# A four-layer attention and gated-MLP kernel: 17 query blocks over one unpadded token axis, and the bulk weights moved to another DMA queue and a later time

## Chip, cores, metric

One NeuronCore of a Trainium2 chip. The metric is device time in microseconds (us), median of several executions without the profiler. Profiles are of one separate execution each; their span is close to the timed figure, except where said. "Landing" is the moment when the last byte of a transfer has arrived; the "granted clock" is the share of its full rate at which PE was allowed to run.

KB is 1024 bytes, as the profile counts. Engine names in the profile: PE is the matrix engine, PEld its weight loads, DVE the vector engine, ACT the scalar engine, POOL and SP the others. Loads are issued by SP or ACT into that engine's own DMA queue.

## The reference

Four layers on 2048 tokens of width 448, in bf16: attention (A), gated MLP (B), A, B, each with a layernorm before it and a residual after it. The code is shortened here.

```python
def _A_ref(x, wqkv, wo):            # 16 heads of 28; each token sees itself and 7 others, 2 apart
    ...
    off = jnp.arange(8) * 2
    idx = pos[:, None] - off[None, :]          # keys pos, pos-2, ..., pos-14
    ...                                        # gather, scale, mask idx < 0, softmax, weighted sum
    return o @ wo

def _B_ref(x, w_gate, w_up, w_down):           # 448 -> 1792 -> 448
    return ((x @ w_gate) * (x @ w_up)) @ w_down

x = x + _A_ref(_layernorm(x), A_wqkv, A_wo)
x = x + _B_ref(_layernorm(x), B_w_gate, B_w_up, B_w_down)
x = x + _A_ref(_layernorm(x), A_wqkv, A_wo)
x = x + _B_ref(_layernorm(x), B_w_gate, B_w_up, B_w_down)
```

## The kernel before

Tokens are reordered (even ones, then odd ones), so that "2 apart" becomes "next to each other" inside each half of 1024. The work is cut into 16 blocks of 128 tokens and 4 chunks of 512. A static scheduler inside the kernel program takes all operations with their dependencies, priorities and estimated durations, and fixes one order for each engine. Each engine gets its operations in that order, and one that waits holds up those behind it (SP's 25.2 us below are a case).

The attention of a half runs in query blocks of at most 120, each with 8 keys in front, over an axis with 16 columns of padding before each half (cuts marked by dots, comments added, the settings of the last line gathered from several):

```python
QB, NQP, NQB, PAD = 120, 9, 18, 16
...
def qb_info(qb):
    r, k = divmod(qb, NQP)
    t0 = QB * k
    nq = min(QB, HALF - t0)                    # the ninth block of a half has 64 queries
    return r, k, t0, nq, nq + 8, HALF * r + t0
...
PE_T = ("00", "01")                            # layer 0, chunks 0 and 1: transposed by PE; the rest by DMA
HEAD_P = (-30.0, -29.5, -29.0, -28.5)          # priorities of the four chunks' layernorms of layer 0
HOLD_BA, LN1, ATT_P, A_CAP = 3000.0, (4,), 1.1, 6
```

The three MLP weights (1568 KB each) are loaded once, from SP, right after the small weights:

```python
for nm, lo, src in (("wg", 0, B_w_gate), ("wu", 64, B_w_up)):
    plain_dma("sp", WGU[lo:lo + 64, :, :], src.rearrange("(k p) f -> p k f", p=64), nm, f"d_{nm}", lat=26000.0, prio=-44)
plain_dma("sp", WD[:], B_w_down.rearrange("(c p) e -> p c e", p=128), "wd", "d_wd", lat=30000.0, prio=-43)
```

Chunks 2 and 3 of layer 0 are transposed by DMA, also from SP. In layer 0 these transposes wait until the last weight (`wd`) has landed:

```python
# xn_sb: the normalised block (a ring of 6 slots);  X: its transpose, xnTa
sc.add("sp", one(lambda E, ...: E.dma_start_transpose(X[:, :, c0:c0 + 128], xn_sb[:, slot, 0:128 * nt]), ("T", li, B)),
       1300.0, deps=[("xn", li, B)] + war + ([f"c_p0", "c_p1"] if par == 0 else []) + (["wd"] if li == 0 else []), ...)
```

From xnTa come Q and K (weights WQK) and V (weights WV); then scores, exponential (ACT, into E_sb), mask (DVE), weighted sum, normalisation, output projection. MLP matmuls read xnTb and WGU, then hT and WD. Most matmuls run as pairs, each on half of PE's rows.

The softmax here doesn't subtract the row's maximum and nothing guards it: scores larger than these inputs give would overflow.

## Time and profile before

| | before |
|---|---|
| time | 411.28 us (410.95 to 411.81, 4 runs beside those of the changed kernel) |
| span of the first profile | 814.9 us: PE at half rate in that execution |
| span of a second profile, taken with the experiments | 410.0 us: PE at full rate |
| PE busy in the second profile | 397.1 us (97%) |

The page, first two lines (span, then busy time of each engine, share of the span, and instructions):

```profile
span 814.9 us, 10679 instructions
...
PE 805.7 (99%) x4682; PEld 280.6 (34%) x4682; DVE 283.2 (35%) x561; ACT 213.6 (26%) x338; POOL 5.4 (1%) x21
```

The span is twice the timed figure, and PE is busy for 99% of it, longer than a timed execution takes in all. So the PE durations of this profile are useless for the timed run. SP's waits (what it waited for: us in all, times, longest) and then the page's DMA issues (queue, KB each, median us from issue to landing) of the same profile:

```profile
SPq L345 <- DMA WD<-in_B_w_down_dram: 25.2, 1, 25.2
```

```profile
WGU<-in_B_w_gate_dram SPq DMA_DIRECT2D x1, 1568.0 KB, 14.2
WGU<-in_B_w_up_dram SPq DMA_DIRECT2D x1, 1568.0 KB, 22.3
WD<-in_B_w_down_dram SPq DMA_DIRECT2D x1, 1568.0 KB, 26.0
...
xnTa<-xn_sb SPq DMA_TRANSPOSE x24, 2.5
```

SP stands still for 25.2 us on WD, and then transposes that land in 2.5 us each. It looks like 25 us to be gained. But it is SP that waits, and the question is whether PE needs those transposes earlier. The half-rate profile can't tell, as its PE is late for everything. The second profile of the same kernel answers: first its busy line, then PE's timeline around the spot (start, us, instructions; in brackets the idle time before, if any, and what ended it), then the transposes in a window around the head (shortest/median/longest issue in ns, first and last start):

```profile
PE 397.1 (97%) x4682; PEld 194.2 (47%) x4682; DVE 277.3 (68%) x561; ACT 209.9 (51%) x338; POOL 5.4 (1%) x21
```

```profile
49.00 0.33 PE L700 MATMUL ps<-qk 28*72 28x64 bf16 x16 [0.60 <-ACT E_sb L707]
49.27 6.36 PE L580 MATMUL ps<-xnTa,WQK 64*128 64x512 bf16 x56
...
64.35 1.69 PE L795 MATMUL ps<-xnTb,WGU 64*128 64x512 bf16 x14
```

### The profile page before, as it was taken

The page shows a single profiled execution, that of the slowest core. Times are in us where ns is not written, and L with a number is a line of the kernel's source. Part 1 is how long each engine was busy: PE and PEld are TensorE (multiplying, and loading weights), DVE is VectorE, ACT ScalarE, POOL GpSimd, SP SyncE. Part 2 cuts the span into 40 slices and gives each one's busy share as a digit, 9 for nine tenths or more (in the row PEclk, how much of TensorE's full clock was granted, in tenths as well). Part 3 has the DMA queues.
Part 4 walks back from the last instruction along what each step waited for, and adds up shares of the span by engine and source line. Part 5 has one row for each costly group of instructions (what it writes and reads, how often), then busy time and mean ns, then how long its engine had stood idle before and what let it go on. Part 6 is the DMA issues. An engine that isn't in the chain of part 4 may idle for free.

```text
span 814.9 us, 10679 instructions
## 1 busy us (share of the span) xinstructions
PE 805.7 (99%) x4682; PEld 280.6 (34%) x4682; DVE 283.2 (35%) x561; ACT 213.6 (26%) x338; POOL 5.4 (1%) x21
## 2 busy tenths in 40 slices
PE   9999999999999999999999999999999999999998
PEld 5323333333233333333333333333333333333333
DVE  5346335335522334333442343423234332211211
ACT  2465334421221213322142321323114101100110
POOL 2000000000000000000000000000000000000000
DMA  9811103000300201000310002100030020000000
GB/s 253 176 27 23 37 0 46 2 1 8 64 0 1 46 1 27 1 1 1 46 27 1 1 1 46 27 1 0 7 63 2 1 57 12 0 1 23 1 0 23
DMA packets 51750, 21.44 MB, mean 26 GB/s; under 512 B 43576, under 2 KB 50808, under 8 KB 51704
## 3 DMA queue, kind: packets, MB, share of 16 engines
q1 hardware_dynamic: 50984, 19.78, 12.1%
q8 instruction: 37, 0.61, 0.3%
q10 hardware_dynamic: 720, 0.98, 0.3%
q14 instruction: 9, 0.07, 0.0%
HBM read 8.43 MB, written 1.84 MB: 13 GB/s over the span
## 4 chain that ended last, share of the span: by engine, by line
PE 99%; DVE 1%; ACT 0%; issue 0%
PE ps L795 45%; PE ps L596 27%; PE ps L580 19%; PE ps L731 2%; PE ps L700 2%; PE ps L816 1%; PE ps L466 1%; PE ps L543 0%; DVE E_sb L713 0%; PE ps L727 0%; DVE x_sb L768 0%; DVE v_sb L680 0%; DVE st L513 0%; ACT E_sb L707 0%; DVE oT L751 0%
## 5 line engine op out<-in xcount | busy, mean ns | idle before, releaser
L795 PE MATMUL ps<-xnTb,WGU 64*128 64x512 bf16 x1568 | 373.9, 671 | 1.3 <-ACT E_sb L707 1.1
L795 PEld LDWEIGHTS ps<-xnTb,WGU 64*128 64x128 bf16 x1568 | 115.8, 142 | 230.8 <-issue 225.8
L596 PE MATMUL ps<-WD,hT 64*128 64x448 bf16 x840 | 177.4, 617 | 0.1
L801 ACT ACTIVATE g_sb<-ps 128x512 bf16<-128x512 f32 x112 | 66.8, 597 | 355.0 <-PE ps L795 354.9
L804 DVE TENSOR_TENSOR hT<-g_sb,ps 128x512 bf16<-128x512 bf16 x112 | 76.7, 685 | 219.5 <-ACT g_sb L801 219.4
L580 PE MATMUL ps<-xnTa,WQK 64*128 64x512 bf16 x448 | 108.8, 672 | 0.1
L596 PEld LDWEIGHTS ps<-WD,hT 64*128 64x128 bf16 x840 | 63.6, 147 | 102.1 <-issue 100.0
L768 DVE TENSOR_TENSOR x_sb<-x_sb,ps 128x448 bf16<-128x448 bf16 x62 | 36.2, 615 | 138.0 <-PE ps L596 138.0
L707 ACT ACTIVATE E_sb<-ps 128x960 bf16<-128x960 f32 (+1 forms) x72 | 64.4, 926 | 29.3 <-PE ps L700 29.1
L596 PE MATMUL ps<-wo_g,oT 64*128 64x448 bf16 x256 | 58.5, 603 | 0.9 <-DVE oT L751 0.8
L580 PE MATMUL ps<-WV,xnTa 64*128 64x448 bf16 (+1 forms) x280 | 56.4, 550 | 0.5
L580 PEld LDWEIGHTS ps<-xnTa,WQK 64*128 64x128 bf16 x448 | 32.4, 142 | 64.0 <-issue 59.6
L713 DVE TENSOR_TENSOR E_sb<-E_sb,MK 128x960 bf16<-128x960 bf16 (+1 forms) x72 | 44.3, 628 | 22.2 <-ACT E_sb L707 22.1
L631 ACT ACTIVATE qk<-ps 128x1024 bf16<-128x1024 f32 x24 | 24.5, 1023 | 77.6 <-PE ps L580 77.6
L513 DVE BATCH_NORM_STATS2 st<-x_sb 128x6 f32<-128x448 bf16 x64 | 37.1, 612 | 3.3 <-DMA x_sb<-in_A_x_dram 3.3
L534 DVE TENSOR_SCALAR xn_sb<-x_sb,mv,rstd 128x512 bf16<-128x512 bf16 (+1 forms) x64 | 32.9, 572 | 6.4 <-ACT rstd L518 6.4
L596 PEld LDWEIGHTS ps<-wo_g,oT 64*128 64x128 bf16 x256 | 17.3, 129 | 36.2 <-issue 33.3
L580 PEld LDWEIGHTS ps<-WV,xnTa 64*128 64x128 bf16 (+1 forms) x280 | 17.5, 127 | 34.3 <-issue 26.6
L742 ACT ACTIVATE R_sb<-R_sb 128x480 f32<-128x480 f32 (+1 forms) x32 | 18.4, 574 | 37.8 <-DVE R_sb L740 37.8
L680 ACT ACTIVATE v_sb<-ps 128x896 bf16<-128x896 f32 (+1 forms) x16 | 13.2, 822 | 48.0 <-PE ps L580 48.0
L751 DVE TENSOR_TENSOR oT<-ps,R_sb 128x480 bf16<-128x480 f32 (+1 forms) x36 | 22.3, 622 | 5.5 <-ACT R_sb L744 5.4
L740 DVE LOAD_MASK_SELECT R_sb<-ps x32 | 0.4, 14 | 64.5 <-PE ps L731 64.5
(45 smaller groups left out, 191.9 us busy)
## 6 DMA issues: line engine op xcount, KB each, us to landing
x_sb<-in_A_x_dram SPq DMA_DIRECT2D x4, 448.0 KB, 6.8
out_dram<-x_sb SPq DMA_DIRECT2D x15, 112.0 KB, 1.7
WGU<-in_B_w_gate_dram SPq DMA_DIRECT2D x1, 1568.0 KB, 14.2
WGU<-in_B_w_up_dram SPq DMA_DIRECT2D x1, 1568.0 KB, 22.3
WD<-in_B_w_down_dram SPq DMA_DIRECT2D x1, 1568.0 KB, 26.0
hT<-in_A_wqkv_dram ACTq DMA_DIRECT2D x4, 224.0 KB, 5.3
xnTb<-xn_sb SPq DMA_TRANSPOSE x32, 3.0
WV<-in_A_wqkv_dram SPq DMA_DIRECT2D x4, 112.0 KB, 5.4
```

The costliest lines, as they stand in the source:

```text
L513: sc.add("dve", one(lambda E, B=B: E.bn_stats(st6[:, B, :], x_sb[:, B, :]), ("bn", li, B)), 525.0, deps=[("x", li - 1, B)] + ([("xn", li - ...
L534: sc.add("dve", one(lambda E, B=B, dst=dst, src=src: E.tensor_scalar(dst, src, mv[:, B, 0:1], rstd[:, B:B + 1], ALU.subtract, ALU.mult), ( ...
L580: parts[0 if s < 3 else 1][1].append((lambda E, w=w, c=c, lo=lo, st=st, sp_=sp_: E.matmul(u["out"](w), u["lhs"](w, c, lo, lo + 64), u["rhs ...
L596: ins.append((lambda E, w=w, c=c, lo=lo, st=st, sp_=sp_: E.matmul(outs(w), lhs(w, c, lo), rhs(w, c, lo), start=st, stop=sp_), keys[w] if s ...
L631: return E.activation(dst, src, ACT.Copy) if hasattr(E, "activation") else E.tensor_copy(dst, src)
L707: return E.activation(E_sb[0:nk, slot, 2 * hp:2 * hp + 2, 0:4 * nq], ps[0:nk, b0:b0 + 2, 0:4 * nq], ACT.Exp, scale=SCALE)
L713: return E.tensor_tensor(e, e, m, ALU.mult)
L751: return E.tensor_tensor(oT[:, :, t0:t0 + nq], ps[:, bk[0], 0:4 * nq].rearrange("p (h n) -> p h n", h=4), R_sb[:, rs, 0:4 * nq].rearrange( ...
L768: sc.add("dve", one(lambda E: E.tensor_tensor(x_sb[:, B, :], x_sb[:, B, :], ps[:, bk[w], 0:D], ALU.add), ("x", li, B)), dve_est(D), deps=[ ...
L795: ins.append((lambda E, u=u, k=k, w=w: E.matmul(u["out"](w), WGU[64 * w:64 * w + 64, k, 128 * u["fc"]:128 * u["fc"] + 128], X[64 * w:64 * ...
L801: sc.add("act", one(lambda E, gs=gs, bk=bk: E.activation(g_sb[:, gs, :], ps[:, bk[0], :], ACT.Copy), ("G", li, j, fc)), act_est(512), deps ...
L804: sc.add("dve", one(lambda E, gs=gs, bk=bk, fc=fc: E.tensor_tensor(hT[:, fc, hs, :], g_sb[:, gs, :], ps[:, bk[1], :], ALU.mult), ("H", li, ...
```

## The change

Three things at once:

1. **17 query blocks** per attention layer over one axis of 2048 tokens without padding: the first of 128 queries, then 16 of 120, one of which straddles the middle and gets a mask of its own (and its last multiply cut in two). 28 V matmuls fewer, pads and their memsets gone.
2. **Bulk weights on ACT's queue, later.** They are gated on the normalisation of block 11, the last of chunk 2, so that chunk 2's transposes may go first. The transposes don't wait for `wd` any more. The intent is to bring chunk 2's transposes forward by a dozen us.
3. **Settings** of the scheduler: layernorms of chunks 2 and 3 at later priorities (the lowest number goes first), finer layernorm groups, a smaller lead for attention in the order (`ATT_P`), and two limits of the scheduler.

```diff
-HEAD_P = (-30.0, -29.5, -29.0, -28.5)
+HEAD_P = (-30.0,-29.5,-19.3,-18.8)
-HOLD_BA = 3000.0
+HOLD_BA = 2000.0
-LN1 = (4,)
+LN1 = (1,1,2)
-ATT_P = 1.1
-A_CAP = 6
+ATT_P = 0.6
+A_CAP = 5
 ...
 def qb_info(qb):
-    r, k = divmod(qb, NQP)
-    t0 = QB * k
-    nq = min(QB, HALF - t0)
-    return r, k, t0, nq, nq + 8, HALF * r + t0
+    if qb == 0:
+        return 0, 128, 0, 128
+    tok = 128 + QB * (qb - 1)
+    return tok - 8, 128, tok, QB
 ... (masks, buffers without pads, the straddling block: cut)
+    GATE = [("x", -1, 15)] if "02" in PE_T else [("xn", 0, 11)]
     for nm, lo, src in (("wg", 0, B_w_gate), ("wu", 64, B_w_up)):
-        plain_dma("sp", WGU[...], ..., nm, f"d_{nm}", lat=26000.0, prio=-44)
-    plain_dma("sp", WD[:], ..., "wd", "d_wd", lat=30000.0, prio=-43)
+        plain_dma("act", WGU[...], ..., nm, f"d_{nm}", deps=GATE, lat=12000.0 if lo == 0 else 20000.0, prio=-44)
+    plain_dma("act", WD[:], ..., "wd", "d_wd", deps=GATE, lat=26000.0, prio=-43)
 ...
-        1300.0, deps=[("xn", li, B)] + war + ([f"c_p0", "c_p1"] if par == 0 else []) + (["wd"] if li == 0 else []), ...
+        1300.0, deps=[("xn", li, B)] + war, ...
```

More of the change, by code (lines that the diff above doesn't have):

```diff
@@ L19 @@
 QB = 120
-NQP = 9
-NQB = 2 * NQP
-PAD = 16
-SEG = PAD + HALF
-CP = 2 * SEG
+NQB = 17
+EW = 4 * 128
 SCALE = DH ** -0.5
@@ L30 @@
 MAIN = "R64"
-PE_T = ("00", "01")
+PE_T = ("00","01")
 HEAD_LN = 4
-HEAD_P = (-30.0, -29.5, -29.0, -28.5)
+HEAD_P = (-30.0,-29.5,-19.3,-18.8)
 HOLD_A = 500.0
-HOLD_BA = 3000.0
+HOLD_BA = 2000.0
 HOLD_BB = 0.0
@@ L42 @@
 POOL_WQK = True
-LN0 = (2, 2)
-LN1 = (4,)
+LN0 = (2,2)
+LN1 = (1,1,2)
 VFIRST = False
@@ L49 @@
 JITTER = 0.0
-ATT_P = 1.1
-A_CAP = 6
+ATT_P = 0.6
+A_CAP = 5
 B_CAP = 8
 SEQ = "A00 A01 B10 A02 B11 A03 B12 A20 B13 A21 B30 A22 B31 A23 B32 B33".split()
-def col(tok):
-    return PAD + tok + (PAD if tok >= HALF else 0)
 def qb_info(qb):
-    r, k = divmod(qb, NQP)
-    t0 = QB * k
-    nq = min(QB, HALF - t0)
-    return r, k, t0, nq, nq + 8, HALF * r + t0
+    if qb == 0:
+        return 0, 128, 0, 128
+    tok = 128 + QB * (qb - 1)
+    return tok - 8, 128, tok, QB
+STRADDLE = next(q for q in range(NQB) if qb_info(q)[2] < HALF < qb_info(q)[2] + qb_info(q)[3])
 class Op:
@@ L391, in build @@
     eps_sb = sb([128, 1], dt.float32, "eps_sb")
-    xnT = {0: sb([128, 4, CP], bf, "xnTa"), 1: sb([128, 7, 1024], bf, "xnTb")}
-    qk = sb([128, 2, 4, CP], bf, "qk")
+    xnT = {0: sb([128, 4, S], bf, "xnTa"), 1: sb([128, 7, 1024], bf, "xnTb")}
+    qk = sb([128, 2, 4, S], bf, "qk")
     WQK = sb([128, 4, 2, 512], bf, "WQK")
@@ L399, in build @@
     v_sb = sb([128, NV, 512], bf, "v_sb")
-    E_sb = sb([128, NE, 4, 480], bf, "E_sb")
-    R_sb = sb([128, NR, 480], dt.float32, "R_sb")
+    E_sb = sb([128, NE, 4, EW], bf, "E_sb")
+    R_sb = sb([128, NR, EW], dt.float32, "R_sb")
     g_sb = sb([128, NG, 512], bf, "g_sb")
@@ L405, in build @@
     ones32 = sb([128, 32], bf, "ones32")
-    MK = sb([128, 2, QB], bf, "MK")
+    MK = sb([128, 3, 128], bf, "MK")
     ident = sb([128, 128], bf, "ident")
@@ L452, in build @@
     sc.add("pool", one(lambda E: E.memset(WQK[:].rearrange("p c w (h e) -> p (c w h) e", e=32)[:, :, DH:32], 0.0), "c_wqk0"), 700, prio=-45)
-    memset("pool", xnT[0][:, :, 0:PAD], 0.0, "c_p0", 150)
-    memset("pool", xnT[0][:, :, SEG:SEG + PAD], 0.0, "c_p1", 150)
     sc.add("pool", one(lambda E: E.memset(v_sb[:].rearrange("p s (h e) -> p (s h) e", e=32)[:, :, DH:32], 1.0), "c_v"), 400, prio=-40)
-    memset("pool", qk[:, :, :, 0:PAD], 0.0, "c_p2", 200)
-    memset("pool", qk[:, :, :, SEG:SEG + PAD], 0.0, "c_p3", 200)
     memset("pool", MK[:], 1.0, "i_mk0", 300)
-    sc.add("pool", one(lambda E: E.affine_select(MK[:, 0, :], MK[:, 0, :], [[-1, QB]], ALU.is_ge, 0.0, base=-1, channel_multiplier=1), "i_mk1"), 300, deps=["i_mk0"], prio=-40)
-    sc.add("pool", one(lambda E: E.affine_select(MK[:, 0, :], MK[:, 0, :], [[1, QB]], ALU.is_ge, 0.0, base=W, channel_multiplier=-1), "i_mk2"), 300, deps=["i_mk1"], prio=-40)
-    sc.add("pool", one(lambda E: E.affine_select(MK[:, 1, :], MK[:, 0, :], [[0, QB]], ALU.is_ge, 0.0, base=-8, channel_multiplier=1), "c_mk"), 300, deps=["i_mk2"], prio=-40)
+    sc.add("pool", one(lambda E: E.affine_select(MK[:, 0, :], MK[:, 0, :], [[-1, 128]], ALU.is_ge, 0.0, base=7, channel_multiplier=1), "i_mk1"), 300, deps=["i_mk0"], prio=-40)
+    sc.add("pool", one(lambda E: E.affine_select(MK[:, 0, :], MK[:, 0, :], [[1, 128]], ALU.is_ge, 0.0, base=0, channel_multiplier=-1), "c_mk0"), 300, deps=["i_mk1"], prio=-40)
+    sc.add("pool", one(lambda E: E.affine_select(MK[:, 1, :], MK[:, 1, :], [[-1, 128]], ALU.is_ge, 0.0, base=-1, channel_multiplier=1), "i_mk2"), 300, deps=["i_mk0"], prio=-39)
+    sc.add("pool", one(lambda E: E.affine_select(MK[:, 1, :], MK[:, 1, :], [[1, 128]], ALU.is_ge, 0.0, base=W, channel_multiplier=-1), "c_mk1"), 300, deps=["i_mk2"], prio=-39)
+    qx, kx = HALF - qb_info(STRADDLE)[2], HALF - qb_info(STRADDLE)[0]
+    sc.add("pool", one(lambda E: E.tensor_copy(MK[:, 2, :], MK[:, 1, :]), "i_mk3"), 300, deps=["c_mk1"], prio=-38)
+    sc.add("pool", one(lambda E: E.affine_select(MK[:, 2, qx:], MK[:, 2, qx:], [[0, 128 - qx]], ALU.is_ge, 0.0, base=-kx, channel_multiplier=1), "c_mk2"), 300, deps=["i_mk3"], prio=-38)
     memset("pool", ones32[:], 1.0, "c_ones", 100)
@@ L481, in build @@
         plain_dma("sp", dst, src, ("wo", j), "d_wo", deps=["c_wo"], lat=12000.0, prio=-45)
+    GATE = [("x", -1, 15)] if "02" in PE_T else [("xn", 0, 11)]
     for nm, lo, src in (("wg", 0, B_w_gate), ("wu", 64, B_w_up)):
-        plain_dma("sp", WGU[lo:lo + 64, :, :], src.rearrange("(k p) f -> p k f", p=64), nm, f"d_{nm}", lat=26000.0, prio=-44)
-    plain_dma("sp", WD[:], B_w_down.rearrange("(c p) e -> p c e", p=128), "wd", "d_wd", lat=30000.0, prio=-43)
+        plain_dma("act", WGU[lo:lo + 64, :, :], src.rearrange("(k p) f -> p k f", p=64), nm, f"d_{nm}", deps=GATE, lat=12000.0 if lo == 0 else 20000.0, prio=-44)
+    plain_dma("act", WD[:], B_w_down.rearrange("(c p) e -> p c e", p=128), "wd", "d_wd", deps=GATE, lat=26000.0, prio=-43)
     WO = [("wo", j) for j in range(4)]
@@ L525, in ln_chunk @@
                 dst = xn_sb[:, slot, 0:512].rearrange("p (a n) -> p a n", a=2)
-                c0 = col(128 * B)
+                c0 = 128 * B
                 war = readersA.get((li - 2, B), [])
@@ L537, in ln_chunk @@
                 sc.add("sp", one(lambda E, slot=slot, c0=c0: E.dma_start_transpose(X[:, :, c0:c0 + 128], xn_sb[:, slot, 0:128 * nt]), ("T", li, B)),
-                       1300.0, deps=[("xn", li, B)] + war + ([f"c_p0", "c_p1"] if par == 0 else []) + (["wd"] if li == 0 else []), dma=f"d_t{par}_{j}", mode=li, lat=1400.0 if par == 0 else 1900.0, prio=prio)
+                       1300.0, deps=[("xn", li, B)] + war, dma=f"d_t{par}_{j}", mode=li, lat=1400.0 if par == 0 else 1900.0, prio=prio)
             else:
@@ L601, in qk_chunk @@
         X = xnT[0]
-        c0 = col(512 * j)
+        c0 = 512 * j
         tdeps = [("T", li, B) for B in range(4 * j, 4 * j + 4)]
@@ L607, in qk_chunk @@
             for qb in range(NQB):
-                r, k, t0, nq, nk, tok = qb_info(qb)
-                if tok - 8 < hi and tok + nq > lo:
+                k0, nk, tok, nq = qb_info(qb)
+                if k0 < hi and tok + nq > lo:
                     war.append(("S", li - 2, qb))
@@ L633, in qk_chunk @@
             sc.add(("act", "dve"), one(mk(None), ("QK", li, j, c)), {"act": act_est(1024), "dve": dve_est(1024)},
-                   deps=[("Kps", li, j, c), ("Qps", li, j, c)] + war + ["c_p2", "c_p3"], release=[(bk, 0), (bk, 1)], prio=prio)
+                   deps=[("Kps", li, j, c), ("Qps", li, j, c)] + war, release=[(bk, 0), (bk, 1)], prio=prio)
         for B in range(4 * j, 4 * j + 4):
@@ L651, in v_group @@
         infos = [qb_info(q) for q in qbs]
-        for r, k, t0, nq, nk, tok in infos:
-            lo = max(t0 - 8, 0) + HALF * r
-            for B in range(lo // 128, (tok + nq - 1) // 128 + 1):
+        for k0, nk, tok, nq in infos:
+            for B in range(k0 // 128, (k0 + nk - 1) // 128 + 1):
                 blocks.add(B)
-        tdeps = [("T", li, B) for B in sorted(blocks)] + [p for _, p in slots if p is not None] + ["c_p0", "c_p1"]
+        tdeps = [("T", li, B) for B in sorted(blocks)] + [p for _, p in slots if p is not None]
         split = len(qbs) == 1
@@ L660, in out @@
         def out(which):
-            return ps[0:infos[0 if split else which][4], bk[which], 0:nv]
+            return ps[:, bk[which], 0:nv]
         def lhs(which, dc, lo, hi):
-            r, k, t0, nq, nk, tok = infos[0 if split else which]
-            c0 = col(tok) - 8
-            return X[lo:hi, dc, c0:c0 + nk]
+            k0, nk = infos[0 if split else which][:2]
+            return X[lo:hi, dc, k0:k0 + nk]
         def rhs(which, dc, lo, hi):
@@ L671, in v_group @@
         s0 = slots[0][0]
-        nk = infos[0][4]
+        nk = infos[0][1]
         def fn(E):
@@ L686, in attn_front @@
     def attn_front(li, qb, prio):
-        r, k, t0, nq, nk, tok = qb_info(qb)
-        ck = col(tok) - 8
-        cq = col(tok)
-        jl = (max(t0 - 8, 0) + HALF * r) // 512
+        ck, nk, cq, nq = qb_info(qb)
+        tok = cq
+        mi = 0 if qb == 0 else 2 if qb == STRADDLE else 1
+        jl = ck // 512
         jh = (tok + nq - 1) // 512
@@ L694, in attn_front @@
         bk = Banks(4, pair=True)
-        if (li > 0 or jh >= S_AFTER) and qb % NQP:
+        if (li > 0 or jh >= S_AFTER) and qb:
             deps = deps + [("E", li, qb - 1, 0), ("E", li, qb - 1, 1)]
@@ L711, in fm @@
                 e = E_sb[0:nk, slot, 2 * hp:2 * hp + 2, 0:4 * nq].rearrange("p b (h n) -> p b h n", h=4)
-                m = MK[0:nk, 1 if k == 0 else 0, 0:nq].unsqueeze(1).unsqueeze(1).to_broadcast([nk, 2, 4, nq])
+                m = MK[0:nk, mi, 0:nq].unsqueeze(1).unsqueeze(1).to_broadcast([nk, 2, 4, nq])
                 return E.tensor_tensor(e, e, m, ALU.mult)
             by_pool = hp == 1 and li == 0 and jh < POOL_MASK
-            sc.add(("dve", "pool") if by_pool else "dve", one(fm, ("E", li, qb, hp)), {"dve": dve_est(8 * nq, 2.0, 60.0), "pool": 2.2 * 8 * nq}, deps=[("Ex", li, qb, hp), "c_mk"], prio=prio)
+            sc.add(("dve", "pool") if by_pool else "dve", one(fm, ("E", li, qb, hp)), {"dve": dve_est(8 * nq, 2.0, 60.0), "pool": 2.2 * 8 * nq}, deps=[("Ex", li, qb, hp), f"c_mk{mi}"], prio=prio)
         return slot
     def attn_back(li, qb, slot, prio):
-        r, k, t0, nq, nk, tok = qb_info(qb)
+        k0, nk, tok, nq = qb_info(qb)
         by_pe = li == 0 and (tok + nq - 1) // 512 < D_PE
@@ L745, in attn_back, with fn @@
                deps=[("Rl", li, qb)], prio=prio)
-        if r == 1:
-            war = [("Y", li, B - 8) for B in range(tok // 128, (tok + nq - 1) // 128 + 1)]
-        else:
-            war = [("Y", li - 2, B + 8) for B in range(tok // 128, (tok + nq - 1) // 128 + 1)] if li >= 2 else []
-        def fn(E):
-            return E.tensor_tensor(oT[:, :, t0:t0 + nq], ps[:, bk[0], 0:4 * nq].rearrange("p (h n) -> p h n", h=4),
-                                   R_sb[:, rs, 0:4 * nq].rearrange("p (h n) -> p h n", h=4), ALU.mult)
-        sc.add("dve", one(fn, ("N", li, qb)), dve_est(4 * nq), deps=[("AV", li, qb), ("R", li, qb)] + war, release=[(bk, 0)], prio=prio)
+        war = []
+        for B in range(tok // 128, (tok + nq - 1) // 128 + 1):
+            if B >= 8:
+                war.append(("Y", li, B - 8))
+            elif li >= 2:
+                war.append(("Y", li - 2, B + 8))
+        cut = [tok] + [HALF] * (tok < HALF < tok + nq) + [tok + nq]
+        ins = []
+        for a, z in zip(cut, cut[1:]):
+            def fn(E, a=a, z=z):
+                return E.tensor_tensor(oT[:, :, a % HALF:a % HALF + z - a], ps[:, bk[0], 0:4 * nq].rearrange("p (h n) -> p h n", h=4)[:, :, a - tok:z - tok],
+                                       R_sb[:, rs, 0:4 * nq].rearrange("p (h n) -> p h n", h=4)[:, :, a - tok:z - tok], ALU.mult)
+            ins.append((fn, ("N", li, qb) if z == cut[-1] else None))
+        sc.add("dve", ins, dve_est(4 * nq, fixed=70.0 * len(ins)), deps=[("AV", li, qb), ("R", li, qb)] + war, release=[(bk, 0)], prio=prio)
     def y_blocks(li, B, prio):
@@ L758, in y_blocks @@
         for qb in range(NQB):
-            r, k, t0, nq, nk, tok = qb_info(qb)
+            _, _, tok, nq = qb_info(qb)
             if tok < 128 * (B + 2) and tok + nq > 128 * B:
@@ L835, in qbs_of @@
     def qbs_of(j):
-        r = j // 2
         res = []
-        for qb in range(NQP * r, NQP * (r + 1)):
-            _, k, t0, nq, nk, tok = qb_info(qb)
+        for qb in range(NQB):
+            _, _, tok, nq = qb_info(qb)
             if (tok + nq - 1) // 512 == j:
@@ L859, in back @@
                 lo, hi = 128 * B, 128 * (B + 2)
-                cov = [q for q in range(NQB) if qb_info(q)[5] < hi and qb_info(q)[5] + qb_info(q)[3] > lo]
+                cov = [q for q in range(NQB) if qb_info(q)[2] < hi and qb_info(q)[2] + qb_info(q)[3] > lo]
                 if B not in d[1] and all(q in d[0] for q in cov):
```

## The prediction

> **What bounds the kernel now.** The profiled execution spans 814.9 us, twice the timed 411.4 us, with PE busy 99%. In the timeline, 182 gate/up matmuls take 42.7 us: 467 ns per row-tiled pair of 512 columns. The Trainium skill ("TensorE: Matmul & The Clock Gate", Part 1) gives 426.7 ns for 512 columns cold and 215.7 warm. So PE ran at about half speed under the profiler (though it prints clock 1.0), and the timed runs must be warm. I keep DVE, ACT and DMA durations and halve PE's.
>
> From the table of stretches: from the first V matmul (14.1 us) to the first gate/up matmul (105.7 us) PE is busy 87.6 us, so about 44 us warm; DVE is busy 45.6 and ACT 42.9. In this head all three need about the same time, so latencies can show. After it PE has about 705 us (353 warm) against some 232 of DVE and 166 of ACT: PE-bound. Halving everything from 14.1 us on, plus an 11 us start and a 2.4 us end, gives about 413. Hence few us of stall are left to win; the warm rate is unseen, so perhaps up to 15, mostly in the head.
>
> **What the change does.**
> 1. 17 query blocks per attention layer instead of 18. Query columns stay 2048, so score, value and mask columns stay. V projection loses one split group per layer: 14 matmuls of 224 columns, 1.8 us in the trace, 0.8 us warm, twice: **-1.6 us** of PE. The order has 4590 matmuls instead of 4682, and 121 mode changes both times. One block's fixed costs on ACT and DVE go (under 1 us per layer). Pads and their memsets were off the path.
> 2. Bulk weights. Now issued from SP at 8.6 to 10.8 us, landing 14.2, 22.3 and 26.0 us later; SP then waits 25.2 us for WD, to 36.1 us, and only then sends chunk 2's transposes (1.3 us each to issue, 2.5 to land: about 43 us). After: they wait for chunk 2's normalised block 11 (about 21-23 us, counting DVE work), on ACT's queue. Transposes land near 30 instead of 43 us; weights land near 40-49 us. The first gate/up matmul should come near 55-60 us in both, so no starvation. The wait on WD was mostly hidden: before, chunk 2's QK sits in PE order behind attention of chunks 0-1, whose ACT work (about 35 us from 10 us on) ends at 45-48 us. I give this **-1 to -4 us**.
> 3. Finer LayerNorm groups: some 60 more small ACT instructions (0.2-0.3 us, about 14 us busy in all). Earlier first transposes, but 3-4 us more ACT in the head: **0 to +2 us**. The other settings reorder the PE-bound middle: **-2 to +1 us**.
>
> **Prediction.** 407.5 us, 80% range 401 to 412. Faster by over 2%: 0.18; within 2%: 0.78; slower by over 2%: 0.04.
>
> **What would show it.** Chunk 2's transposes issued at 20-30 us in time order; WD landing at 40-50 us; no gate/up matmul waiting on weights; 28 fewer V matmuls. A gain over 6 us would mean real stalls on WD's wait.
>
> **What would make it wrong.** A warm rate near 216 ns per pair with 15 or more us of stalls removed (faster, 395-402); transposes slowed by sharing the DMA engines with weights (the skill's "DMA: Bandwidth & Descriptors", "Issuing engines are not separate DMA queues"), or weights late for chunk 0's gate/up (slower).

## More of the kernel before

```profile
L537 SPq DMA_TRANSPOSE xnTa<-xn_sb x8: 1191/1267/2226, 36.3 to 51.7; - x8
...
DMA to landing us min/median/max: 2.5/2.5/4.1
```

In the second profile, taken with the experiments and with PE at full rate (span 410.0 us), the transposes start at 36.3 us, and chunk 2's Q/K matmuls begin at 49.27 us, straight after the attention work ahead of them, without a wait. In the list of all that PE waited for (what: us in all, times, longest) no DMA of xnTa stands; this is its first line, the costliest:

```profile
PE ps L700 <- ACT E_sb L707: 1.8, 2, 1.2
```

SP's 25 us are hidden. The whole execution has 410.0 - 397.1 = 12.9 us of idle PE, and that is all that any change of order or of loads could win.

The stretch from the first matmuls to the end of the head, and the long middle (columns: window, its length, then busy us and instructions of PE, PEld, DVE, ACT, POOL, then the granted PE clock, the DMA share and GB/s), same profile:

```profile
10.20:80.00 69.80, 64.11 (x853) 29.80 (x852) 57.52 (x127) 52.11 (x80) 0.00 (x0) 0.95 0.60 119
...
80.00:405.00 325.00, 321.36 (x3745) 154.98 (x3742) 212.81 (x417) 153.61 (x250) 0.00 (x0) 1.00 0.16 31
```

After 80 us PE is busy 99% of the time. Before that PE, DVE and ACT all have a lot to do, and waits can show.

## The result, and the profile after

| | before | after |
|---|---|---|
| time, median of 4 runs | 411.28 us (410.95 to 411.81) | **423.66 us** (422.60 to 424.82) |
| ratio, 95% interval | | 1.030 [1.027, 1.033]: slower |
| span of the profile | 410.0 us (second profile) | 420.8 us |
| PE busy | 397.1 us | 395.2 us |
| idle PE | 12.9 us | 25.6 us |

PE has a little less to do, and the time is 12 us longer. The busy line of the page after, and its slices of PE and of the granted PE clock (tenths, 40 slices of 10.5 us):

```profile
PE 395.2 (94%) x4590; PEld 188.6 (45%) x4590; DVE 279.5 (66%) x556; ACT 216.8 (52%) x385; POOL 5.7 (1%) x20
...
PE   8980898699999999999999999999999999999997
...
PEclk9995799899999999999999999999999999999999
```

The fourth slice of PE is empty. PE's timeline shows what it waited for:

```profile
20.19 0.81 PE L578 MATMUL ps<-xnTa,WQK 64*128 64x512 bf16 x6
...
30.26 0.74 PE L578 MATMUL ps<-WV,xnTa 64*128 64x448 bf16 x6 [0.17 <-ACT E_sb L703]
43.32 1.47 PE L578 MATMUL ps<-xnTa,WQK 64*128 64x512 bf16 x6 [12.32 <-DMA xnTa<-xn_sb]
...
80.07 2.42 PE L797 MATMUL ps<-xnTb,WGU 64*128 64x512 bf16 x14 [1.93 <-DMA xnTb<-xn_sb]
...
385.86 21.32 PE L797 MATMUL ps<-xnTb,WGU 64*128 64x512 bf16 x196
```

PE runs dry at 31.0 us and waits 12.3 us for the transposes of chunk 2, the very ones that the change wanted to bring forward. They let it go on at 43.3 us, which is where the prediction had placed them for the kernel *before*. Six matmuls of the same form that took 0.81 us at 20.2 us take 1.47 us after the gap.

When were they issued, and when did they land? ACT's timeline, SP's timeline, the transposes in the same window as before, and the page's DMA issues:

```profile
20.15 0.69 ACTq L422 DMA_DIRECT2D WGU<-in_B_w_gate_dram  x1
20.88 0.64 ACTq L422 DMA_DIRECT2D WGU<-in_B_w_up_dram  x1
21.55 0.64 ACTq L422 DMA_DIRECT2D WD<-in_B_w_down_dram  x1
```

```profile
19.18 27.07 SPq L535 DMA_TRANSPOSE xnTa<-xn_sb  x8
```

```profile
L535 SPq DMA_TRANSPOSE xnTa<-xn_sb x8: 1190/1364/7725, 19.2 to 45.0; - x8
...
DMA to landing us min/median/max: 2.6/12.2/19.9
```

```profile
WGU<-in_B_w_gate_dram ACTq DMA_DIRECT2D x1, 1568.0 KB, 10.8
WGU<-in_B_w_up_dram ACTq DMA_DIRECT2D x1, 1568.0 KB, 19.0
WD<-in_B_w_down_dram ACTq DMA_DIRECT2D x1, 1568.0 KB, 24.6
```

Read them together. The four transposes of chunk 2 were issued at 19.2, 20.5, 21.9 and 23.3 us, far earlier than before. The first landed after 2.6 us. The next three took 17.2, 19.4 and 19.9 us (single records of the trace). The weights were issued between 20.15 and 22.2 us: after the *normalisation* of block 11, as coded, which is the moment when only the first of the four transposes had left. A transpose takes SP about 1.3 us to issue, so chunk 2's transposes did not go first, as was the intent: three of four went out beside 4704 KB of weights.

The gap and what it costs, in the same two stretches as before and in the gap itself (a DMA share above 1 is as the tool prints it):

```profile
10.20:80.00 69.80, 50.39 (x692) 21.69 (x692) 48.29 (x104) 46.24 (x82) 0.00 (x0) 0.90 0.53 109
...
31.00:43.30 12.30, 0.00 (x2) 0.01 (x1) 1.55 (x3) 1.50 (x5) 0.00 (x0) 0.58 1.13 227
...
80.00:405.00 325.00, 322.50 (x3718) 152.85 (x3720) 221.05 (x430) 164.68 (x293) 0.00 (x0) 0.99 0.16 32
```

Up to 80 us PE did 64.11 - 50.39 = 13.7 us less work than before. Of that, 1.9 us is work that it no longer has, and 1.1 us is made good in the middle (322.5 against 321.4), which leaves 10.7 us; the spans differ by 10.8. So all of the loss lies before 80 us, and the middle is as it was. In the gap the other engines stand still too: ACT and DVE have 1.5 us of work each, DVE being held for 10.2 us because the normalised blocks that it wants to overwrite are still being read by those transposes.

### The profile page after: what moved, and what is told of

Read it like the earlier page. It is cut to its first block, busy times and chain, and to the rows that moved or that the text cites. A ratio compares the mean times of both kernels' runs of the same rounds, so it can differ in the third digit from the quotient of the medians. Undisturbed runs are those within 1.5% of the kernel's fastest.

```text
span 420.8 us, 10554 instructions
## 1 busy us (share of the span) xinstructions
PE 395.2 (94%) x4590; PEld 188.6 (45%) x4590; DVE 279.5 (66%) x556; ACT 216.8 (52%) x385; POOL 5.7 (1%) x20
## 4 chain that ended last, share of the span: by engine, by line
PE 87%; DMA 7%; ACT 3%; DVE 2%; issue 1%; SPq 0%
PE ps L797 39%; PE ps L594 24%; PE ps L578 16%; DMA xnTa<-xn_sb 6%; PE ps L727 2%; PE ps L463 2%; PE ps L696 2%; PE ps L818 1%; ACT E_sb L703 1%; DMA xnTb<-xn_sb 1%; ACT qk L629 1%; ACT g_sb L803 1%; PE ps L541 1%; DVE hT L806 0%; DVE x_sb L770 0%
## 5 line engine op out<-in xcount | busy, mean ns | idle before, releaser
L797 PE MATMUL ps<-xnTb,WGU 64*128 64x512 bf16 x1568 | 180.0, 378 | 3.3 <-DMA xnTb<-xn_sb 1.9
L797 PEld LDWEIGHTS ps<-xnTb,WGU 64*128 64x128 bf16 x1568 | 75.6, 94 | 91.9 <-issue 4.1
L594 PE MATMUL ps<-WD,hT 64*128 64x448 bf16 x840 | 84.7, 349 | 0.3
L703 ACT ACTIVATE E_sb<-ps 128x960 bf16<-128x960 f32 (+1 forms) x68 | 64.2, 973 | 10.1 <-PE ps L696 8.0
L578 PE MATMUL ps<-xnTa,WQK 64*128 64x512 bf16 x448 | 55.0, 382 | 13.4 <-DMA xnTa<-xn_sb 13.0
L594 PEld LDWEIGHTS ps<-WD,hT 64*128 64x128 bf16 x840 | 40.4, 94 | 38.9 <-PE ps L594 0.5
L709 DVE TENSOR_TENSOR E_sb<-E_sb,MK 128x960 bf16<-128x960 bf16 (+1 forms) x68 | 43.6, 654 | 12.9 <-ACT E_sb L703 12.5
L532 DVE TENSOR_SCALAR xn_sb<-x_sb,mv,rstd 128x512 bf16<-128x512 bf16 (+1 forms) x64 | 34.6, 574 | 10.4 <-DMA xnTa<-xn_sb 10.2
L752 DVE TENSOR_TENSOR oT<-ps,R_sb 128x480 bf16<-128x480 f32 (+3 forms) x36 | 22.2, 621 | 12.8 <-ACT R_sb L740 12.7
L578 PE MATMUL ps<-WV,xnTa 64*128 64x448 bf16 (+1 forms) x252 | 29.2, 347 | 1.1 <-ACT qk L629 0.5
L594 PE MATMUL ps<-wo_g,oT 64*128 64x448 bf16 x256 | 29.4, 350 | 0.6 <-ACT E_sb L703 0.4
L738 ACT ACTIVATE R_sb<-R_sb 128x480 f32<-128x480 f32 (+1 forms) x30 | 18.0, 600 | 22.3 <-DVE R_sb L736 22.2
L740 ACT ACTIVATE R_sb<-R_sb 128x480 f32<-128x480 f32 (+1 forms) x34 | 20.6, 604 | 0.5
L736 DVE STREAM_SHUFFLE R_sb<-ps 128x480 f32<-128x480 f32 (+1 forms) x30 | 20.6, 693 | 0.0
## 6 DMA issues: line engine op xcount, KB each, us to landing
WGU<-in_B_w_gate_dram ACTq DMA_DIRECT2D x1, 1568.0 KB, 10.8
```

Of the source, the lines that this page charges most:

```text
L532: sc.add("dve", one(lambda E, B=B, dst=dst, src=src: E.tensor_scalar(dst, src, mv[:, B, 0:1], rstd[:, B:B + 1], ALU.subtract, ALU.mult), ( ...
L578: parts[0 if s < 3 else 1][1].append((lambda E, w=w, c=c, lo=lo, st=st, sp_=sp_: E.matmul(u["out"](w), u["lhs"](w, c, lo, lo + 64), u["rhs ...
L594: ins.append((lambda E, w=w, c=c, lo=lo, st=st, sp_=sp_: E.matmul(outs(w), lhs(w, c, lo), rhs(w, c, lo), start=st, stop=sp_), keys[w] if s ...
L703: return E.activation(E_sb[0:nk, slot, 2 * hp:2 * hp + 2, 0:4 * nq], ps[0:nk, b0:b0 + 2, 0:4 * nq], ACT.Exp, scale=SCALE)
L709: return E.tensor_tensor(e, e, m, ALU.mult)
L752: return E.tensor_tensor(oT[:, :, a % HALF:a % HALF + z - a], ps[:, bk[0], 0:4 * nq].rearrange("p (h n) -> p h n", h=4)[:, :, a - tok:z - ...
```

## Experiments

My theory (T): the transposes share the DMA engines with the bulk weights on unfavourable terms, and that alone makes the loss. Rivals: the new order (17 blocks, settings) puts PE's work badly (R1); the move to ACT's queue, or the time ACT spends on it, is at fault (R2); the weights come late for the MLP (R3). R3 falls on the profile after alone: of PE's waits none is for WGU or WD, and the weights land at 31, 40 and 46 us, the first gate/up matmul runs at 80. Half of R2 falls with ACT's timelines: ACT spends 2 us on issuing the loads, but its first exponential starts only 0.8 us later than in after_sp3 below (22.24 against 21.41 us). The expectations below are quoted as written before each run; each call of runs had its own runs of the kernel before beside it.

### 1. The kernel before, again

No edit; one look, to get a profile at full rate.

> The kernel before, unchanged, run again to get a profile with PE at full rate (the one shown before ran at half rate). All theories: 411 us. If WD's wait was hidden before, as my prediction had it, PE shows no gap above 3 us before chunk 2's first QK matmul. If not, a gap of 5 us or more that ends on a DMA of xnTa near 40 to 43 us, and a stall total of about 15 to 20 us before the first gate/up matmul[...].

411.71 us (one run), span 410.0, granted clock 0.992. This is the second profile shown above. It confirms that the wait for WD was hidden, and that 12.9 us of idle PE was all there was.

### 2. One part of the change at a time

**W**: the kernel before with only the weights moved (and `wd` dropped from the transposes' waits). **BS**: the changed kernel with only the weights put back. Both are reordered by the kernel's own scheduler.

```diff
 # W, on the kernel before
-    plain_dma("sp", WGU/WD ...)                      # three loads
+    GATE = [("xn", 0, 11)];  plain_dma("act", WGU/WD ..., deps=GATE)
-    deps=[...] + (["wd"] if li == 0 else [])         # of the transposes
+    deps=[...]
 # BS, on the changed kernel: the reverse
```

> Only the bulk weights' part of the change, in the kernel before (18 blocks, old settings). Theory 1 (chunk 2's DMA transposes share the DMA engines with 4.7 MB of weights issued after the second of them, and PE waits for them): transposes of chunk 2 land 10 us or later after issue, PE idles 8 us or more on them, 418 to 426 us. Theory 2 (the slowdown is the new settings or the 17 blocks, and the wait only covers other waits): within 2 us of 411.

> The change without the weights' part: 17 blocks and new settings, weights first on SP and transposes behind WD, as before. Theory 1: about as before, 408 to 413 us, transposes of chunk 2 landing in 2.5 to 4 us each from 36 us on. Theory 2: 418 us or more.

W: 430.35 us (429.64 to 430.55, 4 runs), ratio to before 1.0458 [1.0429, 1.0486]. BS: 410.18 us (409.31 to 411.01), 0.9963 [0.9926, 1.0]. PE's wait in W, and W's transposes:

```profile
PE ps L581 <- DMA xnTa<-xn_sb: 15.7, 2, 15.4
```

```profile
L538 SPq DMA_TRANSPOSE xnTa<-xn_sb x8: 1190/1337/8019, 20.8 to 46.7; - x8
...
DMA to landing us min/median/max: 2.5/12.1/20.0
```

The weights part alone makes the loss, with the same kind of wait (15.4 us) on the old blocks and old settings; W came out even above the 418 to 426 us that I had expected. Without it the rest is level with before, as expected. R1 falls as the cause of the 12 us.

**B**: only the 17 blocks (old settings, old weights). **S**: only the settings, on the kernel before.

```diff
 # B, on the changed kernel with the weights put back: old HEAD_P, HOLD_BA, LN1, ATT_P, A_CAP
 # S, on the kernel before: the new HEAD_P, HOLD_BA, LN1, ATT_P, A_CAP
```

> Only the 17 blocks without padding, in the kernel before (old settings, old weights). My prediction gave them -1.6 us of PE work: 408 to 411 us; a rival that the fewer, uneven blocks cost more than they save: 412 us or more. With the run BS (410.2) this also tells what the settings do: B minus BS.

> Only the new settings, in the kernel before (18 blocks, weights first on SP). If the settings gain by themselves what they gave beside the 17 blocks (4.6 us): 405 to 408.5 us, faster than both kernels. If they only mend the order of the 17-block kernel: 410 to 413 us.

B: 414.81 us (414.45 to 415.98, 6 runs), 1.0095 [1.0074, 1.0115]. S: 411.67 us (411.18 to 412.26, 6 runs), 0.9999 [0.998, 1.0018]. The busy line of B:

```profile
PE 394.1 (95%) x4590; PEld 189.9 (46%) x4590; DVE 276.9 (67%) x553; ACT 209.1 (51%) x328; POOL 5.7 (1%) x20
```

The 17 blocks take 3.0 us of PE work away (397.1 to 394.1; I had costed 1.6), and yet the time rises by some 4 us: idle PE grows from 12.9 to 18.6 us (span 412.7), in several waits for ACT and DVE, the longest single one 1.3 us. The settings alone do nothing. Together with the 17 blocks they bring 414.8 down to 410.2: they mend the order that the 17 blocks spoil (B and BS are of different rounds, each beside its own runs of the kernel before). Why the scheduler's order with 17 blocks and old settings stalls more was not pursued further; only its waits are seen.

### 3. Same order on every engine, weights moved in time or to the other queue

Here the changed kernel is scheduled as it is, and afterwards the three loads are moved, so that all other instructions keep their order. **after_sp2**: on SP, behind chunk 2's last transpose. **after_sp3**: on SP, behind chunk 3's last. **after_late**: still on ACT, but after its eighth exponential and waiting for chunk 3's last transpose.

```diff
     sc.schedule()
+    moved = [op for op in sc.order["act"] if op.dma in ("d_wg", "d_wu", "d_wd")]
+    for op in moved:
+        sc.order["act"].remove(op)
+        op.deps = []
+    at = max(i for i, op in enumerate(sc.order["sp"]) if op.dma == "d_t0_2" and op.mode == 0) + 1   # sp3: d_t0_3
+    sc.order["sp"][at:at] = moved
 # after_late: op.deps = [("T", 0, 15)]; put back into sc.order["act"] behind ("Ex", 0, 3, 1)
```

> The changed kernel with every engine's order kept, except that the three weight loads leave ACT's queue and stand in SP's queue right after the four transposes of chunk 2. Theory 1: those four land by about 28 us, PE's gap of 12.3 us at 31 us goes; chunk 3's transposes now stand behind the weights and land near 46 to 50 us, so some 3 to 6 us of stall come back there; 410 to 416 us. Theory 2: no change, 421 us or more.

> The changed kernel with every engine's order kept; the three weight loads stand in SP's queue behind all eight transposes of chunks 2 and 3. Theory 1: all eight transposes land within 4.5 us of issue, weights are issued at about 37 us and WD lands near 62 us; the first gate/up matmul comes at 62 to 67 us; no PE wait on xnTa above 2 us: 407 to 412 us. Rival (the new order has other stalls that the wait covered): 415 us or more.

> The changed kernel with every engine's order kept except that the three weight loads, still on ACT's queue, wait for the landing of all of chunks 2's and 3's transposes and stand behind the eighth exponential of ACT (about 39 us). Theory 1 (only the time at which the bulk starts beside the transposes matters, not the queue): transposes land in 2.5 to 4.5 us, no PE wait on xnTa above 1 us, within 2 us of the run with the weights behind the transposes on SP (410.1): 408 to 413 us. Rival (ACT's queue is itself the cost): 415 us or more.

| | time, us | ratio to before | longest PE wait for xnTa |
|---|---|---|---|
| changed kernel | 423.66 | 1.030 [1.027, 1.033] | 12.3 |
| after_sp2 | 421.02 (420.57 to 421.43) | 1.0234 [1.0206, 1.0261] | 9.7 |
| after_sp3 | 410.12 (409.95 to 411.36) | 0.9976 [0.9942, 1.0011] | 0.6 |
| after_late | 412.23 (411.21 to 412.89) | 1.0022 [0.9999, 1.0046] | 0.6 |

PE's wait for xnTa in the changed kernel and in after_sp3:

```profile
PE ps L578 <- DMA xnTa<-xn_sb: 13.0, 2, 12.3
```

```profile
PE ps L578 <- DMA xnTa<-xn_sb: 0.6, 1, 0.6
```

The transposes and the head's stretch of after_sp3 (the stretch ends at its first gate/up matmul), then the transposes of after_late:

```profile
L535 SPq DMA_TRANSPOSE xnTa<-xn_sb x8: 1190/1265/1889, 19.2 to 36.4; - x8
...
DMA to landing us min/median/max: 2.4/2.5/4.2
```

```profile
10.20:67.10 56.90, 48.59 (x692) 21.23 (x693) 49.34 (x105) 47.53 (x84) 0.00 (x0) 0.98 0.67 134
```

```profile
L535 SPq DMA_TRANSPOSE xnTa<-xn_sb x8: 1190/1264/1590, 19.0 to 35.9; - x8
...
DMA to landing us min/median/max: 2.4/2.5/4.2
```

The same transposes in the same order, without bulk beside them, land in 2.5 us. after_sp3 does its 692 head matmuls by 67.1 us; the changed kernel needed until 80.0 for as many. after_late has the loads on ACT, as the change has, and is level with the kernel before. So it is the time at which the loads go out, not their queue: R2 falls.

after_sp2 was expected at 410 to 416 and missed. PE's timeline and SP's timeline of it show why:

```profile
51.47 4.31 PE L578 MATMUL ps<-xnTa,WQK 64*128 64x512 bf16 x20 [9.70 <-DMA xnTa<-xn_sb]
```

```profile
19.14 5.22 SPq L535 DMA_TRANSPOSE xnTa<-xn_sb  x4
...
28.76 20.55 SPq L535 DMA_TRANSPOSE xnTa<-xn_sb  x4
```

Chunk 2's four transposes are out in 5.2 us and PE doesn't wait for them. But chunk 3's four now stand behind the weights in the same queue, their issue is stretched over 20.6 us (a single one takes 16.6 us), and PE waits 9.7 us for *them*. I had seen that they would be late and underrated by how much.

The same move on other versions: **W_sp3** (on W), **BW_sp3** (on the 17 blocks with old settings), **WS_sp3** (on the kernel before with the new settings).

> The kernel W (18 blocks, old settings, transposes not behind WD), with the three loads in SP's queue behind the eight transposes of chunks 2 and 3. Theory 1: W's 430.4 falls by its waits on xnTa (15.7 us) and a clock restart of 1 to 3 us to 410 to 415 us. If the old order has other stalls once the transposes come early: 418 us or more.

> Candidate to beat both: 17 blocks, old settings, loads on SP behind the eight transposes. If the new settings only cost (60 more small ACT instructions in the head), 404 to 408 us; if they are neutral, 408 to 411 us like the same with new settings.

> New settings, 18 blocks, loads in SP's queue behind the eight transposes of chunks 2 and 3. If early transposes are worth anything of themselves, it is below S by 1 us or more; if WD's wait was hidden, within 1.5 us of S either way. No PE wait on xnTa above 2 us.

W_sp3: 411.80 us (411.74 to 412.04, 4 runs), 1.0015 [0.9995, 1.0035]. BW_sp3: 415.26 (414.42 to 415.71, 6 runs), 1.0097 [1.0079, 1.0115]. WS_sp3: 413.13 (411.30 to 414.79, 6 runs), 1.0038 [1.0012, 1.0064]. Compare each with its twin with early weights: before, B (1.0095), S (0.9999). Transposes that go out some 15 us earlier, undisturbed, gain nothing on any of the three. W_sp3 and WS_sp3 came out as expected; BW_sp3, the candidate to beat both kernels, lies above both of its expected ranges (404 to 411 us), as does B. The expected gain never existed, as the wait for WD was off PE's path to begin with.

### 4. How the transposes and the bulk share

Each transfer in the trace has a size and a queue. SP's queue carries the transposes, as records of 256 bytes (512 for one transpose); ACT's carries gate and up as records of 3584 bytes and down as records of 896. Records begun in each stretch of the changed kernel (this is a count over the trace's transfers; the 4-byte records that both queues also have are in the totals):

```
us       SP's queue, all      ACT's queue, all (of them 3584 B, 896 B)
20-22          544                12  (12, 0)
22-25            0               184  (184, 0)
25-26           15                59  (59, 0)
26-30          227               225  (210, 0)
30-34          196               192  (191, 0)
34-38          213               219  (219, 0)
38-42          869               869  (21, 832)
42-46         1674               976  (0, 960)
```

From 26 to 42 us the two queues start nearly equally many records in each stretch, as if they took turns. Each 256-byte record has to pay for one of 3584 bytes, until WD's rows come at 38 us. From 34 to 38 us that is some 45 KB of transposes (181 records of 256 bytes, the rest of 4) against 767 KB of weights. Alone, the transposes move 1344 records in 3 us (after_sp3, 22 to 25 us, 448 per us); beside gate and up about 50 per us, a ninth. The weights hardly notice: 61 records per us alone (22 to 25 us here), some 52 when shared. An estimate from these numbers: the three transposes have 1536 records, at 50 per us that is 30 us, less what they gain once WD's small records come at 38 us. They took until 43.

The Trainium skill ("DMA: Bandwidth & Descriptors", "Queues, rings and completion order") says that each DMA engine goes round-robin between the queues for which it has work, a whole packet of descriptors at a time. The counts agree with equal turns. Whether a turn is one record or a packet of equally many, and what hands out the turns, can't be told from counts.

If turns are counted in records, thinner rows of the bulk should let the transposes through sooner. **after_wd1** sends WD (896-byte rows) first. **after_thin** cuts gate and up into four loads each, of 448 columns, so that all rows have 896 bytes. Both are on ACT at the same place.

```diff
     sc.schedule()
 # after_wd1: the three places on ACT refilled as WD, gate, up
+    for i, op in zip(at, [loads[2], loads[0], loads[1]]):
+        acts[i] = op
 # after_thin: gate and up as four DMAs each
+    for q in range(4):
+        dst = WGU[lo:lo + 64, :, 448 * q:448 * q + 448]
+        src = w.rearrange("(k p) f -> p k f", p=64)[:, :, 448 * q:448 * q + 448]
```

> The changed kernel with every engine's order kept; only WD (rows of 896 B) is loaded before gate and up (rows of 3584 B). Theory 1a (the engines alternate one packet of each queue: between 26 and 38 us of the trace after, 256 B transpose packets and 3584 B weight packets were 227 and 225, 196 and 192, 213 and 219 in each 4 us): three blocks of chunk 2 (1536 packets) alternate with 896 B packets at about 870 pairs in 4 us, so they land by 28 to 30 us instead of 38 to 43, and PE's gap at 31 us shrinks below 2 us. Chunk 3's transposes then meet gate and up and land at 45 to 50 us, so 5 to 9 us of stall come back there: 416 to 421 us. Rival 1b (any bulk load in flight holds transposes up, by bytes or until it ends): chunk 2 lands at 38 us or later, gap 8 us or more, 422 to 426 us.

> The changed kernel with every engine's order kept; gate and up are each loaded in four pieces of 448 columns, so that their packets are 896 B instead of 3584 B. Same bytes, same queue, same gate; ACT issues six more DMAs of about 0.65 us, so its exponentials at 22 us come some 4 us later. Theory 1a: chunk 2's transposes land by 30 us and chunk 3's by 42 us beside the weights, no PE wait on xnTa above 2 us; about 3 us of ACT delay remain; 409 to 415 us. Rival 1b: no better than after, plus ACT's delay: 423 us or more.

after_wd1: 424.89 us (423.63 to 426.61), 1.0329 [1.0287, 1.037]. after_thin: 422.07 (420.88 to 422.47), 1.0252 [1.0221, 1.0283]. I expected 416 to 421 and 409 to 415, so both times missed. By the test set beforehand, after_wd1 even came out on the side of the rival 1b (any bulk in flight holds the transposes up): the last of the three landed at 44.2 us, PE's gap was 12.0 us, and the time lies in 1b's 422 to 426. after_thin fits neither (1b: 423 or more). The counts, however, show equal turns again:

```
us       SP's queue   ACT's queue (of them 3584 B, 896 B)
after_wd1
22-25         38           952  (0, 952)
25-26        267           280  (0, 280)
26-30        638           642  (109, 517)
34-38        226           226  (210, 0)
38-42        213           213  (213, 0)
after_thin
30-34        701           701  (0, 676)
```

Where both queues have work, the transposes now get more than 50 records per us: 267 and 277 in the two full us beside WD (25 to 27, after_wd1), 97 to 228 in those beside the thinned gate and up (28 to 34, after_thin). So the rows' size matters, and is not all that does; what else was not followed up. In after_wd1 the three late transposes landed after 7.6, 13.0 and 20.5 us. What spoiled it is that WD had the engines nearly alone for the first 3 us, and more than half of its 1792 small records were gone when the transposes got their turns; then they met the big rows. PE's wait for them stayed at 12.0 us.

In after_thin the three landed after 7.4, 10.9 and 12.4 us, by 36 us instead of 43, and PE did not wait for them. It waited for something else. PE's waits, and ACT's timeline:

```profile
PE ps L578 <- ACT E_sb L703: 10.3, 2, 10.1
```

```profile
20.43 2.82 ACTq L899 DMA_DIRECT2D WGU<-in_B_w_gate_dram  x4
23.27 7.45 ACTq L899 DMA_DIRECT2D WGU<-in_B_w_up_dram  x4
30.76 2.58 ACTq L422 DMA_DIRECT2D WD<-in_B_w_down_dram  x1
33.38 1.94 ACT L703 ACTIVATE E_sb<-ps 128x1024 bf16<-128x1024 f32 x2 [12.43 <-issue]
```

Nine loads in place of three: ACT spent 12.4 us on issuing them, and its exponential, for which PE waits, came that much later. The first four took 0.7 us each, the next four 1.9, the last 2.6. So the cure traded a wait of 12.3 us for one of 10.1, and the experiment tells of the sharing (by the landings and the counts) but not of the time it would have saved.

### 5. No DMA transposes in layer 0's head

**after_pe4** lets PE transpose chunks 2 and 3 of layer 0 too. The gate then becomes the arrival of x, so the weights go out at 12 us with nothing of layer 0 to disturb.

```diff
-PE_T = ("00","01")
+PE_T = ("00","01","02","03")
```

> The changed kernel with chunks 2 and 3 of the first layer transposed by PE like chunks 0 and 1 (the scheduler reorders), weights on ACT's queue once x has landed. No DMA transpose meets the bulk load. Theory 1: no PE wait on xnTa; 32 more PE transposes and 8 more PSUM copies cost 1 to 3 us in the head, the first gate/up matmul no later than 68 us: 407 to 413 us. Rival as for the other: 415 us or more.

416.30 us (414.21 to 419.55, the widest spread of all), 1.0124 [1.006, 1.0188], against an expected 407 to 413: a miss, inside the rival's 415 or more. There is no wait for xnTa by DMA any more, and 7 us of the 12 come back. But the kernel is reordered: its first gate/up matmul comes only at 77.27 us (64.35 in the kernel before), and ACT is held for 5.4 us by issuing the three loads, 1.76 and 1.20 us for the second and third, when PE waits 3.1 us for it. How the rest of the 5 us splits was not followed up.

### What is left as best

after_sp3 (0.9976) and BS (0.9963) lie at the kernel before within their intervals. None of the versions beats both kernels clearly.

## Why the prediction was right or wrong

**Wrong: the size and sign of item 2.** The step that failed is "Transposes land near 30 instead of 43 us", and with it "I give this -1 to -4 us". I took the landing of 2.5 us from the profile before, where the transposes ran alone *because* they waited for WD. With the wait taken away they meet the weights. Measured landing: 17.2 to 19.9 us, PE idle for 12.3 us, and a restart at a lower granted clock (0.58 in the gap; the first six matmuls 1.47 us instead of 0.81). On the old kernel the weights part costs +19.0 us (W, 430.35 against 411.36), on the new one 13.5 (423.66 against BS's 410.18, of other rounds). I named this sharing under "What would make it wrong" and gave all of slower 0.04. I had the two facts side by side that should have raised it: weights issued at 21-23 us and in flight till 40-49, transposes issued 1.3 us apart from about the same moment on.

The wait for WD was more than a wait. It kept two streams apart that get on badly, and it was hidden at no cost. Removing it could win nothing, and lost 12 us.

**Missed: what the gate lets through.** The prediction has the gate right ("they wait for chunk 2's normalised block 11"), but I did not ask how many transposes had left by then. Three of four leave after it.

**Right: the wait on WD was mostly hidden.** It was wholly hidden: no PE wait for xnTa at 49.27 us in the second profile, and W_sp3 at 1.0015. So even with undisturbed transposes the -1 to -4 us were not there.

**Right: PE at half rate in the first profile.** The Trainium skill ("TensorE: Matmul & The Clock Gate", Part 1) gives 215.7 ns for 512 columns warm. In the profile after, 196 matmuls take 21.32 us, 217.6 ns per pair, so the trace agrees within 1%. Idle PE was 12.9 us, within "perhaps up to 15". The middle is PE-bound: 321.4 of 325 us. Wrong in this part: the first gate/up matmul was placed at 55-60 us in both; it came at 64.35 before and 80.07 after.

**Half right: item 1.** 28 fewer V matmuls (252 against 280), 3.0 us less PE work rather than 1.6. But "**-1.6 us** of PE" was booked as time, and B shows some +4 us: a saving on PE counts only if the order stays as tight, and here it did not, until the settings mended it.

**Right by luck: items 1 and 3 together.** Settings alone 0.0 us (S, 0.9999), within item 3's range. But on the 17 blocks the same settings take 4.6 us off (B 414.81, BS 410.18), more than that range allows, and they undo what item 1 had cost. That the sum is small (0.9963), as I had it, is luck: neither part has the size that I gave it there.

**Right: no starvation by weights.** Chunk 2's transposes were issued at 19-24 us, up and WD landed at 40 and 46 us, and no gate/up matmul waited for them. With that, all four signs listed under "What would show it" came about (the first transpose left at 19.2 us), in a kernel that is 3% slower. None of them looked at when the transposes land.

**Open.** Why the bulk has the DMA engines to itself for the first 3 to 4 us (no 256-byte record from 22 to 25 us, though two transposes had been issued); why the order with 17 blocks and old settings has more idle PE; how after_pe4's remaining 5 us divide.

## What to carry to other kernels

A wait that looks wasteful may be what keeps two DMA streams apart: before removing it, list what will then be in flight at the same time, and do not cost a transfer with a landing time that was measured without that company. Small records beside large ones got equal turns here and not equal bytes, so send the small and urgent transfers first, and gate the bulk on their *landing* (or at least the issue of the last one), not on the data that they read. And a gain in front of an engine that isn't waiting is no gain: look at the waits of the engine that bounds the time, at the real clock, before counting the idle time of another.

## What the Trainium skill lacked or had wrong

- "DMA: Bandwidth & Descriptors", "Rules for kernel authors", says that a transpose next to ordinary DMAs needs nothing. That may be meant for correctness (every run here gave the right result), but the cost is missing: landing rose from 2.5 us to 17.2 to 19.9 us beside loads with 3584-byte rows.
- "Advanced Engine Details and Errata", "X-Bar Transpose (TRN2)", says that transposes are as fast as regular DMAs, and nothing of the two side by side. Alone they moved 448 records of 256 bytes per us here (SP issued one transpose per 1.3 us, so this need not be their limit); beside such a load about 50, while the load went on at 52 of its 61 records per us.
- "DMA: Bandwidth & Descriptors", "Queues, rings and completion order", has the round-robin between queues but not what follows from it: equal counts, so that the queue with short rows gets the smaller share of bytes (213 records against 219 from 34 to 38 us, 45 KB against 767 KB).
- The same page, "Issuing engines are not separate DMA queues", calls the time to issue a DMA usually small beside the DMA itself. It was 0.7 us per load at first, but nine loads held ACT for 12.4 us (1.9 us each for the fifth to the eighth, 2.6 for the last), single transposes held SP for 7.7 us (changed kernel) and 16.6 us (after_sp2). I found no page that says that an issue takes longer when much is in flight on the queue, or from what amount on.
- No page that I found explains the first 3 to 4 us in which the bulk alone moved (184 records against 0 from 22 to 25 us).
